# A mixed attention and MLP kernel: transposes moved between token mixing's products, and w4's subtraction moved from POOL to DVE

## The chip, the cores and the metric

One NeuronCore of one Trainium2 chip. The engines are PE (TensorE: products and transposes), ACT (ScalarE), DVE (VectorE), POOL (GpSimd) and SP, whose queue issues the loads. Each takes its instructions in order, and they run beside each other, held together by semaphores. The metric is the device time of one execution in microseconds (us), as the median of several runs.

## The reference

An input x of 2048 tokens by 448 columns goes through two branches, and a gate mixes them per token:

```python
g = _sigmoid((x * gate_w).sum(-1, keepdims=True))
a = _A_ref(x, A_wq, A_wk, A_wv, A_wo)        # 16 query heads of 28, one shared key and value head
b = _B_ref(x, B_w1, B_w2, B_w3, B_w4)
return g * a + (1 - g) * b
```

The branch that matters here is the second one:

```python
h  = _gelu(_layernorm(x) @ w1)                                  # 448 -> 448
hs = concat(four column groups of h, shifted by +1, -1, +2, -2 tokens) @ w2
x1 = x + hs                                                     # token mixing
h2 = _gelu(_layernorm(x1) @ w3) @ w4                            # the MLP, 448 -> 1792 -> 448
return x1 + h2
```

All values are float32.

## The kernel before, in words

**Precision.** PE multiplies in a rounded format. To come close to float32, each operand is kept as two tensors: a high part (names ending in h), a cast by ACT, and a low part (ending in l), which is the raw tensor minus the high part. A product of two operands is three products: high by high, high by low, low by high. So each weight that is loaded goes through the same steps: a DMA into a raw buffer, casts on ACT, a subtraction on DVE or POOL.

**Blocks.** The tokens are four blocks of 512 (`NB` = 4), each of four tiles of 128. The weights w3 and w4 are loaded in seven pairs i = 0 to 6, each of which holds two of the MLP's fourteen hidden chunks f of 128.

**Order.** PE's order is the order of the program. The other engines' order, and that of the loads on SP, is made by a scheduler, which may pull an instruction ahead of others in the program; so an edit of the program's order changes their queues as well.

**The stretch around the change** is the end of the first stage:

- `stage_kv(3)` computes keys and values of the last block, and leaves the values in `vT`. `stage_v(3, vT)` transposes them on PE (tile `vp`); DVE copies the result into `vext` and the gate's sum into `gz`, from which ACT computes `gg` with Exp.
- `ln_begin(0)` takes the statistics of block 0 of x1 on DVE (L126, L127), and POOL makes the factor `rs` (L128, L129).
- `load_w34(i, pool)` loads pair i: `w3raw` (L364), cast by ACT in three pieces (L101, L102, L106), with the low part subtracted by DVE in two (L104, L105); then `w4raw` (L369), cast by ACT (L370) and its low part `w4l` subtracted by POOL (L371). The raw tiles of w3 and of w4 have one buffer each: the load of pair i + 1 cannot start until pair i is cast and subtracted.
- `stage_w2(b)` is token mixing's second product for block b: for each of four tiles t, twelve products into a PSUM tile `hs` of two buffers (L322 to L324), and an addition on DVE that adds it to x1 (L326). It takes a function `between(t)` that is called after each tile.
- `ln_tile(0, t, tp_of)` normalises tile t of block 0: DVE computes `xn` (L135, three buffers), POOL copies its last 64 columns behind it (L137), PE transposes four parts into a PSUM tile `tp` (L140), ACT casts that to `ah` (L109), and DVE makes `al` and a piece of `ah` (L110, L111).

Before the change, block 2's `stage_w2` runs by itself, then come `stage_v(3)`, the loads 1 to 3 in the program's order, the first transposed tile, and block 3's `stage_w2` with the other three transposed tiles between its parts. Those tiles take PSUM buffers of the groups `misc` and `mx`, which have one buffer each.

**Behind the stretch** comes the MLP of block 0. `w3_part(0, f)` makes the product `g_f` (L115 to L119) in a PSUM group `mm` of two buffers; ACT evaluates Gelu on it twice, into `gh` (L409) and `gf` (L410), and DVE makes `gl` from them (L411). So g_2 needs the buffer that `gf_0` frees. `w4_part` (L419 to L421) adds the products with w4 into `acc`, two chunks f later. The loads of pairs 4 to 6 stand at the head of this stage in the program. After the MLP's four blocks comes attention, which takes most of the time and is not touched.

Of the kernel before, what the change touches and what calls it, by code (L numbers as in the profile page):

```python
# [11 lines left out]
ALU = mybir.AluOpType  # L12
# [10 lines left out]
NB = S // 512  # L23
# [12 lines left out]
def f32(ap):  # L36
    return ap.bitcast(F32)
# [3 lines left out]
def gated_mix_kernel(  # L41
# [13 lines left out]
    nc = tc.nc  # L55
# [36 lines left out]
    def misc_tile(name):  # L92
        return psA.tile([P, 512], F32, tag="misc", bufs=1, name=name)
# [5 lines left out]
    def split_w(raw, wh, wl, eng=None):  # L99
        eng = eng or nc.vector  # L100
        nc.scalar.copy(wh[:, 0:3, :], raw[:, 0:3, :])  # L101
        nc.scalar.copy(wh[0:64, 3, :], raw[0:64, 3, :])  # L102
        nc.gpsimd.memset(f32(wh)[64:128, 3, :], 0.0)
        eng.tensor_tensor(wl[:, 0:3, :], raw[:, 0:3, :], f32(wh)[:, 0:3, :], ALU.subtract)  # L104
        eng.tensor_tensor(wl[0:64, 3, :], raw[0:64, 3, :], f32(wh)[0:64, 3, :], ALU.subtract)  # L105
        nc.scalar.copy(wl[64:128, 3, :], raw[64:128, 3, :])  # L106
# [25 lines left out]
    def layernorm_tile(pool, tp_of, b, t, mv, rs, ah, al):  # L132
        xt = x1[:, 4 * b + t, :]
        xn = pool.tile([P, 512], F32, tag="xn", bufs=3, name=f"xn_{pool.name}_{b}_{t}")
        nc.vector.tensor_scalar(xn[:, 0:D], xt, mv[:, t, 0:1], rs[:, t:t + 1],  # L135
                                op0=ALU.subtract, op1=ALU.mult)
        nc.gpsimd.tensor_copy(xn[:, D:512], xn[:, 384:D])  # L137
        tp = tp_of(f"tp_{pool.name}_{b}_{t}").rearrange("p (c n) -> p c n", c=4)
        for c in range(4):
            nc.tensor.transpose(tp[:, c, :], xn[:, c * P:(c + 1) * P], ident)  # L140
        cols = slice(t * P, (t + 1) * P)
        split_a(tp, ah[:, :, cols], al[:, :, cols])
# [60 lines left out]
    with tc.tile_pool(name="s1b", bufs=1) as s1b, \  # L203
# [43 lines left out]
        def stage_kv(b):  # L247
            ah = s1.tile([P, 4, 512], F32R, tag="ah", bufs=2, name=f"ahk_{b}")
            al = s1.tile([P, 3, 512], F32R, tag="al", bufs=2, name=f"alk_{b}")
            if b == 0:  # L250
                for c in range(4):
                    nc.scalar.copy(ah[:, c, :], xraw[b][:, c, :])
                    if c < 3:
                        nc.vector.tensor_sub(al[:, c, :], xraw[b][:, c, :], f32(ah)[:, c, :])
                    else:
                        nc.vector.tensor_sub(ah[64:128, c, :], xraw[b][64:128, c, :], f32(ah)[64:128, c, :])
            else:
                split_a(xraw[b], ah, al)
            xact[b] = (ah, al)
            cols = slice(512 * b, 512 * b + 512)  # L260
            ps = max_tile(f"kv_{b}")[0:64, :]
            proj(ps, kvh, kvl, ah, al)
            nc.scalar.copy(kS[0:32, cols], ps[0:32, :])
            nc.scalar.copy(kS[32:64, cols], ps[0:32, :])
            nc.vector.tensor_sub(kS[64:96, cols], ps[0:32, :], f32(kS)[0:32, cols])
            vT = s1b.tile([32, 512], F32, tag="vT", bufs=1, name=f"vT_{b}")
            nc.scalar.copy(vT, ps[32:64, :])
            return vT

        def stage_v(b, vT):  # L270
            vp = misc_tile(f"vp_{b}")
            for t in range(4):
                nc.tensor.transpose(vp[:, 32 * t:32 * t + 32], vT[:, t * P:(t + 1) * P], ident[0:32, 0:32])
            vp = vp[:, 0:P].rearrange("p (t d) -> p t d", t=4)
            nc.vector.tensor_copy(vext[:, 4 * b:4 * b + 4, 1:1 + DH], vp[:, :, 0:DH])
            nc.vector.tensor_copy(gz[:, 4 * b:4 * b + 4], vp[:, :, DH])
# [40 lines left out]
        def stage_w2(b, between=None):  # L317
            for t in range(4):
                ps = ps1.tile([P, 512], F32, tag="hs", bufs=2, name=f"hs_{b}_{t}")[:, 0:D]
                for m in range(4):  # L320
                    o = 2 + t * P + SHIFTS[m]
                    nc.tensor.matmul(ps, hh[b][0:C, m, o:o + P], w2h[0:C, m, :], start=(m == 0), stop=False)  # L322
                    nc.tensor.matmul(ps, hh[b][0:C, m, o:o + P], w2l[0:C, m, :], start=False, stop=False)
                    nc.tensor.matmul(ps, hl[b][0:C, m, o:o + P], w2h[0:C, m, :], start=False, stop=(m == 3))  # L324
                xt = x1[:, 4 * b + t, :]
                nc.vector.tensor_add(xt, xt, ps)  # L326
                if between:
                    between(t)

        split_w(kvraw, kvh, kvl)  # L330
        vT = stage_kv(0)
# [14 lines left out]
        vT = stage_kv(1)  # L346
# [4 lines left out]
        vT = stage_kv(2)  # L351
        stage_w1(3)
        stage_v(2, vT)
        vT = stage_kv(3)
# [3 lines left out]
        w3h, w3l, w4h, w4l = [], [], [], []  # L358

        def load_w34(i, pool):  # L360
            w3h.append(pool.tile([P, 4, 2 * P], F32R, name=f"w3h_{i}"))
            w3l.append(pool.tile([P, 4, 2 * P], F32R, name=f"w3l_{i}"))
            raw = s2a.tile([P, 4, 256], F32, tag="raw3", bufs=1, name=f"w3raw_{i}")
            nc.sync.dma_start(raw, w3[:, :, i * 256:i * 256 + 256])  # L364
            split_w(raw, w3h[i], w3l[i])
            w4h.append(pool.tile([P, 2, D], F32R, name=f"w4h_{i}"))
            w4l.append(pool.tile([P, 2, D], F32R, name=f"w4l_{i}"))
            raw = s2a.tile([P, 2, D], F32, tag="raw4", bufs=1, name=f"w4raw_{i}")
            nc.sync.dma_start(raw, w4[i * 256:i * 256 + 256, :].rearrange("(c p) n -> p c n", p=P))  # L369
            nc.scalar.copy(w4h[i], raw)  # L370
            nc.gpsimd.tensor_tensor(w4l[i], raw, f32(w4h[i]), ALU.subtract)  # L371

        acts = {}

# [5 lines left out]
        def ln_tile(b, t, tp_of):  # L380
            ah, al, mv, rs = acts[b]
            layernorm_tile(s2a, tp_of, b, t, mv, rs, ah, al)

        ln_begin(0)
        load_w34(0, s2a)
        stage_w2(NB - 2)
        stage_v(3, vT)
        for i in range(1, 4):
            load_w34(i, s2a)
        ln_tile(0, 0, misc_tile)  # L390
        stage_w2(NB - 1, lambda t: ln_tile(0, t + 1, (misc_tile, max_tile)[t % 2]) if t < 3 else None)

    with tc.tile_pool(name="s2", bufs=1, reuse_waits="tile") as s2, \
            tc.tile_pool(name="ps2", bufs=1, space=PSUM, reuse_waits="tile") as ps2:
# [28 lines left out]
        for i in range(4, NF // 2):  # L423
            load_w34(i, s2)
# [385 lines left out]
```

## Time and profile before

| | us |
|---|---|
| median of 3 runs | 1070.64 |
| these runs | 1069.9 to 1074.41 |
| the profiled execution | 1070.98 |
| its span, first to last instruction | 1069.1 |
| mean granted clock of TensorE in it | 0.987 of full speed |
| busy: PE, ACT, DVE, POOL | 1039.7 (97%), 673.2 (63%), 258.0 (24%), 159.8 (15%) |

The profile is of one execution. Its rows name a line of the kernel (L371), the engine, the operation, the tile written and the tiles read. A row of a timeline begins with the start from the span's beginning in us and the duration in us; brackets at its end hold the idle time of the engine before it and what ended that. A row of an operation's summary has durations in ns as minimum, median and maximum. PEld is the loading of PE's weights, SPq is SP's queue of DMA issues. PEclk is the clock that PE was granted as a share of full speed. Numbers of buffers are left out of the names, so `w4l` is each of w4l_0 to w4l_6, and `tp_s2a` is the MLP's transposed tile.

### The profile page before, as it was taken

Reading aid. Unit: us, or ns where it says so; the run is one execution under the profiler, and the core shown is the slowest. Engines: PE = TensorE matmul, PEld = TensorE weight load, DVE = VectorE, ACT = ScalarE, POOL = GpSimd, SP = SyncE. Lnnn points to the kernel's source line nnn. Section 1 sums busy time; section 2 is a strip of 40 time slices with the busy share of each in tenths; the row PEclk is TensorE's granted clock in tenths of the full one; section 3 lists DMA queues with packets and bytes.
Section 4 is the critical chain, followed back from the end, with each engine's and each line's share of the span. In section 5 each row is a group of like instructions: output and inputs, shape, how many; then the busy total and the mean of one; then the engine's idle time right before and its main releaser. Section 6 shows DMA issues by size and latency. Waiting matters only on the chain.

```text
span 1069.1 us, 13948 instructions
## 1 busy us (share of the span) xinstructions
PE 1039.7 (97%) x5610; PEld 679.6 (64%) x5610; DVE 258.0 (24%) x521; ACT 673.2 (63%) x1318; POOL 159.8 (15%) x182
## 2 busy tenths in 40 slices
PE   6999889999999999999999999999999999999995
PEld 4787778888888888454554555554655555555542
DVE  6744952311411311401110110120110210111102
ACT  5444451222222223788888888889888889888873
POOL 5622430110200201603000002010002100000100
PEclk9999899999999999999999999999999999999998
DMA  9401330000000000423211202220202220211001
GB/s 312 131 1 37 111 111 1 1 1 1 1 1 1 1 1 29 164 32 70 33 17 16 31 20 40 39 31 3 39 10 41 39 31 2 40 24 26 10 2 38
DMA packets 30541, 41.15 MB, mean 38 GB/s; under 512 B 8004, under 2 KB 20100, under 8 KB 30340
## 3 DMA queue, kind: packets, MB, share of 16 engines
q1 hardware_dynamic: 30324, 40.04, 16.3%
q8 instruction: 46, 0.75, 0.3%
q14 instruction: 27, 0.22, 0.1%
q10 hardware_dynamic: 144, 0.13, 0.1%
HBM read 23.28 MB, written 3.67 MB: 25 GB/s over the span
## 4 chain that ended last, share of the span: by engine, by line
PE 91%; DVE 4%; DMA 1%; ACT 1%; POOL 1%; issue 1%; SPq 0%; POOLq 0%; ACTq 0%; DVEq 0%
PE s L663 27%; PE pv L625 22%; PE acc L420 4%; PE acc L419 4%; PE acc L421 4%; PE g L115 4%; PE g L116 4%; PE g L117 4%; PE q L503 3%; PE m L166 2%; PE wo L560 1%; PE wo L558 1%; PE wo L556 1%; PE g L119 1%; PE g L118 1%; PE h L116 1%
## 5 line engine op out<-in xcount | busy, mean ns | idle before, releaser
L665 ACT ACTIVATE p<-s 128x512 f32<-128x512 f32 x1024 | 517.6, 627 | 98.1 <-PE s L663 97.8
L663 PE MATMUL s<-qs,kS 98*128 98x512 f32 x1024 | 343.6, 420 | 1.4 <-ACT p L665 0.7
L663 PEld LDWEIGHTS s<-qs,kS 98*128 98x128 f32 x1024 | 181.6, 189 | 168.2 <-ACT p L665 127.1
L625 PE MATMUL pv<-p,vext 128*32 128x512 f32 x2048 | 247.6, 602 | 0.0
L409 ACT ACTIVATE gh<-g 128x512 fp32r<-128x512 f32 x56 | 33.6, 600 | 174.9 <-PE g L119 174.9
L625 PEld LDWEIGHTS pv<-p,vext 128*32 128x32 f32 x2048 | 53.7, 109 | 107.6 <-issue 100.3
L411 DVE TENSOR_TENSOR gl<-gf,gh 128x512 fp32r<-128x512 f32 x56 | 41.3, 738 | 192.1 <-ACT gf L410 192.0
L419 PE MATMUL acc<-w4h,gh 128*128 128x448 f32 x224 | 82.6, 369 | 0.0
L420 PE MATMUL acc<-w4l,gh 128*128 128x448 f32 x224 | 82.0, 366 | 0.0
L421 PE MATMUL acc<-w4h,gl 128*128 128x448 f32 x224 | 81.7, 365 | 0.0
L167 DVE TENSOR_REDUCE mr<-m 128x4 f32<-128x512 f32 x64 | 44.3, 692 | 146.0 <-PE m L166 145.3
L548 POOL CAST onh<-on 128x512 fp32r<-128x512 f32 x15 | 9.2, 614 | 414.8 <-DVE on L545 228.7
L115 PE MATMUL g<-ah,w3h 128*128 128x512 f32 x168 | 67.1, 399 | 3.1 <-ACT gf L410 2.8
L116 PE MATMUL g<-al,w3h 128*128 128x512 f32 x168 | 66.5, 396 | 0.1
L117 PE MATMUL g<-ah,w3l 128*128 128x512 f32 x168 | 66.3, 394 | 0.0
L521 DVE SCALAR_TENSOR_TENSOR good<-rt,good 128x16 f32<-128x16 f32 x15 | 2.6, 175 | 190.2 <-DMA rt<-o 190.2
L419 PEld LDWEIGHTS acc<-w4h,gh 128*128 128x128 f32 x224 | 42.0, 188 | 4.9
L420 PEld LDWEIGHTS acc<-w4l,gh 128*128 128x128 f32 x224 | 42.1, 188 | 4.8
L421 PEld LDWEIGHTS acc<-w4h,gl 128*128 128x128 f32 x224 | 42.0, 188 | 3.6
L166 PEld LDWEIGHTS m<-kS,qs 96*128 96x128 f32 x256 | 38.4, 191 | 6.3 <-DVE mr L167 1.2
L115 PEld LDWEIGHTS g<-ah,w3h 128*128 128x128 f32 x168 | 31.9, 190 | 9.7 <-ACT gf L410 3.3
L564 DVE SCALAR_TENSOR_TENSOR ot<-wo,gg,x 128x448 f32<-128x448 f32 x16 | 10.9, 682 | 108.0 <-PE wo L560 108.0
(204 smaller groups left out, 1144.4 us busy)
## 6 DMA issues: line engine op xcount, KB each, us to landing
qs<-qh SPq DMA_DIRECT2D x32, 256.0 KB
qs<-ql SPq DMA_DIRECT2D x16, 256.0 KB
xq<-in_xT_dram SPq DMA_DIRECT2D x4, 1024.0 KB
x<-in_x_dram SPq DMA_DIRECT2D x4, 896.0 KB
w3raw<-in_w_dram SPq DMA_DIRECT2D x7, 512.0 KB
out_dram<-ot SPq DMA_DIRECT2D x16, 224.0 KB
w4raw<-in_w_dram SPq DMA_DIRECT2D x7, 448.0 KB
xkv<-in_xT_dram SPq DMA_DIRECT2D x3, 1024.0 KB
```

Source lines behind the costliest of these rows:

```text
L115: nc.tensor.matmul(ps, wh[:, c, :], ah[:, c, :], start=(c == 0), stop=False)
L116: nc.tensor.matmul(ps, wh[:, c, :], al[:, c, :], start=False, stop=False)
L117: nc.tensor.matmul(ps, wl[:, c, :], ah[:, c, :], start=False, stop=False)
L166: nc.tensor.matmul(ps[:, j, :], q_of[u][0:96, j, t * P:(t + 1) * P], kS[0:96, 0:MK], start=True, stop=True)
L167: nc.vector.reduce_max(mx_of[u][:, :, t], ps, axis=AX.X)
L411: nc.vector.tensor_sub(gl, gf, f32(gh))
L419: nc.tensor.matmul(ps, gh[:, tok], w4h[i][:, k, :], start=(f == 0), stop=False)
L420: nc.tensor.matmul(ps, gh[:, tok], w4l[i][:, k, :], start=False, stop=False)
L421: nc.tensor.matmul(ps, gl[:, tok], w4h[i][:, k, :], start=False, stop=(f == NF - 1))
L625: nc.tensor.matmul(pv[32 * j:32 * j + 32, :], vext[:, kt, :], ps[j], start=(kt == 0), stop=(kt == NT - 1), tile_position=(0, 32 * j))
L663: nc.tensor.matmul(ps, kS[0:98, kt * P:(kt + 1) * P], q_of[u][0:98, j, :], start=True, stop=True)
L665: nc.scalar.activation(p, ps, AF.Exp, scale=SCALE)
```

## The change

`stage_v(3)` and the four transposed tiles of block 0 move between the products of block 2's `stage_w2`: `stage_v(3)` behind its first tile, transposed tiles 0, 1 and 2 behind the second, third and fourth, and tile 3 right behind that. All four use the group `tp` of two PSUM buffers. Block 3's `stage_w2` then runs by itself, and the loads of pairs 1 to 3 stand behind it in the program. The low parts of all seven pairs of w4 are subtracted by DVE instead of POOL. Nothing that is computed changes.

```diff
@@ load_w34 @@
             nc.scalar.copy(w4h[i], raw)
-            nc.gpsimd.tensor_tensor(w4l[i], raw, f32(w4h[i]), ALU.subtract)
+            nc.vector.tensor_tensor(w4l[i], raw, f32(w4h[i]), ALU.subtract)
@@ end of the first stage @@
         ln_begin(0)
         load_w34(0, s2a)
-        stage_w2(NB - 2)
-        stage_v(3, vT)
+        stage_w2(NB - 2, lambda t: ln_tile(0, t - 1, tp_tile) if t else stage_v(3, vT))
+        ln_tile(0, 3, tp_tile)
+        stage_w2(NB - 1)
         for i in range(1, 4):
             load_w34(i, s2a)
-        ln_tile(0, 0, misc_tile)
-        stage_w2(NB - 1, lambda t: ln_tile(0, t + 1, (misc_tile, max_tile)[t % 2]) if t < 3 else None)
```

The changed kernel is one line shorter, so lines below L390 have numbers lower by one in its profile (Gelu's L409 becomes L408).

## The prediction

> **What bounds the kernel now.** I read the page first, for the engine that ends last, then the list of waits of TensorE from 95 to 260 us, which holds the changed stretch and the MLP's first block, then the chain of work that ended last there, and then each engine's timeline. By the page the chain is PE's:
>
> ```profile
> PE 91%; DVE 4%; DMA 1%; ACT 1%; POOL 1%; issue 1%; SPq 0%; POOLq 0%; ACTq 0%; DVEq 0%
> ```
>
> So this edit can only move the end by moving PE's waits. The list of them (who waited for whom: us in total, times, longest) is short:
>
> ```profile
> PE g L115 <- ACT gf L410: 2.8, 1, 2.8
> PE tp_s2a L140 <- DVE gz L276: 2.7, 1, 2.7
> PE m L166 <- DVE mr L167: 0.5, 2, 0.2
> PE g L115 <- ACT ah L109: 0.3, 1, 0.3
> ```
>
> After the wait for gf_0, PE runs through the MLP's first block. So only the start of the product g_2, which needs the PSUM tile that gf_0 frees, passes to the end; the earlier waits count only if they move gf_0. The chain of waits tells what does (start, us, what):
>
> ```profile
> 124.47 0.84 ACT w4h L370
> 125.39 2.14 POOL w4l L371
> 127.54 3.29 DMA w4raw<-in_w_dram
> 130.88 0.97 issue
> 131.88 2.10 POOL w4l L371
> 134.01 3.34 DMA w4raw<-in_w_dram
> 137.47 0.92 issue
> 138.38 1.28 ACT L409
> 139.68 0.60 ACT gh L409
> 140.28 0.50 ACT gf L410
> 140.82 0.79 PE g L115
> ```
>
> It is the loop of w4's single raw buffer: load, cast on ACT (the "issue" pieces), subtraction on POOL, next load. ACT works in order, and gh_0 and gf_0 stand behind the fifth cast, w4h_4, which began at 137.4. PE, which finished g_1 at 138.0, is early.
>
> **The change, part by part.** The order of instructions of the changed kernel shows ACT's queue as w4h_0, ah_0, ah_1, w3h_1, ah_2, ah_3, w4h_1, w3h_2, w4h_2, w3h_3, table load, gh_0, w4h_3, gf_0. So gf_0 now waits for the fourth pair of weights alone, one w4 round less, and the table load no longer follows the last cast it waits for. From the start of w3h_3 it is casts, table, gh, one w4 cast, gf:
>
> ```profile
> 133.95 0.83 ACT L101 CAST w3h<-w3raw 128x768 fp32r<-128x768 f32 x1 [1.67 <-DMA w3raw<-in_w_dram]
> 134.69 0.40 ACT L102 CAST w3h<-w3raw 64x256 fp32r<-64x256 f32 x1
> 135.12 0.41 ACT L106 CAST w3l<-w3raw 64x256 fp32r<-64x256 f32 x1
> ```
>
> That is 1.6 for the three (133.95 to 135.53), 1.3, 0.5, 0.85 and 0.6, with 0.05 to PE: 4.9 us. The question is when w3raw_3 lands. Against it, w3l_0 moves: on DVE it now stands behind vext, gz and xn_0, and xn_0 waits for rs on POOL.
>
> ```profile
> 109.02 0.94 DVE L104 TENSOR_TENSOR w3l<-w3raw,w3h 128x768 fp32r<-128x768 f32 x1
> 109.88 0.41 DVE L105 TENSOR_TENSOR w3l<-w3raw,w3h 64x256 fp32r<-64x256 f32 x1
> 110.22 0.60 DVE L326 TENSOR_TENSOR x<-x,hs 128x448 f32<-128x448 f32 x1
> 110.86 2.30 DVE L135 TENSOR_SCALAR xn_s2a<-x,mv_s2a,rs_s2a 128x448 f32<-128x448 f32 x1
> ```
>
> ```profile
> 109.01 1.81 POOL L129 TENSOR_TENSOR rs_s2a<-rs_s2a,powt 128x4 f32<-128x4 f32 x1
> ```
>
> ```profile
> L129 POOL TENSOR_TENSOR rs_s2a<-rs_s2a,powt x4: 1007/1007/1813, 109.0 to 202.2; 128x4 f32<-128x4 f32 x4
> ```
>
> Here rs took 1.81 instead of 1.01 while DVE ran L104 and L105, and xn_0 took 2.30 while POOL began its w4l at 110.8: the two engines shut each other out. Without that rs ends at 109.01 + 1.01 = 110.0, xn_0 (448 columns like L326's 0.60, but one input; I take 0.5) at 110.6, L104 and L105 follow with 0.87 + 0.41, and w3raw_0 is free at 111.85 where it was 110.3. The load loop starts 1.55 late.
>
> PE starts the block's first product at 104.58, then vp, then the second product; a product and a transposed tile cost it:
>
> ```profile
> 104.58 0.37 PE L322 MATMUL hs<-w2h,hh 112*128 112x448 f32 x1
> ...
> 126.13 0.60 PE L140 MATMUL tp_s2a<-ident,xn_s2a 128*128 128x128 f32 x4
> 126.48 0.45 PE L322 MATMUL hs<-w2h,hh 112*128 112x448 f32 x1
> ...
> 129.01 0.60 PE L140 MATMUL tp_s2a<-ident,xn_s2a 128*128 128x128 f32 x4
> ```
>
> A tile with its product takes 2.88 (126.13 to 129.01), a product 2.5. PE is at tp_0 at about 110.1 (104.58 + 2 x 2.5 + vp and its wait for vT, half a us) and waits until POOL has copied xn_0's last columns. Between no block by L104 and a full one that copy ends at 110.9 to 112.0; I take 111.9, since L104 starts right behind xn_0. tp_2 then starts at 111.9 + 2 x 2.88 = 117.7, tp_3 at 118.0 and ends at 118.6.
>
> w4l_0 on DVE: the rows of 768 and 256 columns (0.94, 0.41) give 1.04 ns a column, so 896 take 1.07 instead of POOL's 2.1. Seven cost DVE 7.5 us and spare POOL 15. w4l_0 stands behind L326 and three xn, so it ends near 114.7 (111.85 + 0.5 + 3 x 0.45 + 1.07); w4raw_1 follows and, at no more than a w3 load's 4.24 (below), lands at 118.9, when ACT, busy with ah_3 to 119.3, cannot take w4h_1 yet: hidden by 0.4, and past that it would cost what it is late. vp moved ahead of the second product costs PE what it cost behind the fourth, and its wait for vT lies in the wait for xn_0. gg and Exp's table load, now ahead of w4h_0, end that cast at 111.3 (gz at about 108.9, then 1.28, 0.2 and 0.94), 2 us before w4l_0's turn; uncovered they would cost 1.5.
>
> The next w3 round starts late in the same way: DVE takes L105 of w3l_1 behind al and ah of tp_3. ah_3 ends 0.7 after tp_3 (119.3), when one of DVE's two pairs of 0.54 + 0.28 (by that slope) still has 0.3 to go; with the second pair and L105, 120.9. The loads now alternate in SP's queue, w3 ahead of w4; before, it was
>
> ```profile
> 110.36 0.54 SPq L364 DMA_DIRECT2D w3raw<-in_w_dram  x1
> 112.94 7.90 SPq L369 DMA_DIRECT2D w4raw<-in_w_dram  x2
> 120.95 0.55 SPq L364 DMA_DIRECT2D w3raw<-in_w_dram  x1
> ```
>
> ```profile
> 114.60 0.83 ACT L101 CAST w3h<-w3raw 128x768 fp32r<-128x768 f32 x1 [4.88 <-DMA w3raw<-in_w_dram]
> ...
> 126.03 0.83 ACT L101 CAST w3h<-w3raw 128x768 fp32r<-128x768 f32 x1 [0.72 <-DMA w3raw<-in_w_dram]
> ```
>
> A w3 load ahead of its w4 took 4.24 (110.36 to 114.60), one behind it 5.08 (120.95 to 126.03). I take 4.24, as w3 now leads. w3raw_2: issued 120.9, landed 125.15; L101 0.83, L104 0.9, one hs addition 0.5, L105 0.4: w3raw_3 issued 127.9, landed 132.1. Plus 4.9: **g_2 at 137.0, 3.8 before 140.82**. w4_3 is queued behind w3_3: of the pair before, the second w4 issue ended at 120.84 and w3 had landed at 126.03, 5.2 later; I allow 5.6, so 133.5, and w4h_3's turn is at 135.5: covered by 2 us. PE is at g_2 earlier: 129.01 to 138.0 took tp_3, one product, g_0 and g_1; from 118.0 that plus three products more (7.5) is 134.5, so it waits 2.5 us again, and the two waits taken away (2.7, 0.3) gain nothing by themselves. Two new queues stand behind waits. On POOL, the memset of w3h_4 waits for PE's last hs product (about 128.3) and rs of block 1 stands behind it; on DVE block 1's xn and then w3l_3 wait for that rs, to about 132.6 (memsets and rs 2.0, three xn and statistics 2.3): hidden by w3h_3's first cast, at 132.9, and w3l_3 frees only later loads. Behind g_2, DVE has w4l_3 to w4l_6 and w3l_4 to w3l_6 ahead of gl_0 to gl_5. A pair of weights lasts PE two g (5.8, what is left of 129.01 to 138.0 without a tile, a product and the wait of 0.3) and two groups of twelve products like hs's (5.0), and a load round takes 7.0 (120.9 to 127.9): the loads draw ahead by 3.8 a round, which I put at zero cost.
>
> **The clock** is the term that decides. By windows (length; PE, PEld, DVE, ACT, POOL busy; PEclk; DMA, GB/s):
>
> ```profile
> 113.08:116.49 3.41, 1.99 (x12) 1.44 (x10) 3.41 (x11) 1.54 (x3) 1.08 (x3) 1.00 0.71 211
> 116.49:119.91 3.42, 2.14 (x8) 2.04 (x9) 3.42 (x6) 2.85 (x4) 1.89 (x1) 0.51 0.00 1
> 140.39:143.80 3.41, 2.98 (x7) 2.40 (x8) 1.98 (x3) 2.27 (x5) 0.18 (x1) 0.50 0.50 139
> ```
>
> The clock halved after a stretch of 3.41 in which PE was idle 1.42, and again around the gap before g_2, where 2.98 busy us at half clock cost 1.5. The gap that I add at tp_0 lasts 1.8. If these stretches lie at random to it, one of them holds 1.42 of it unless a border falls in its middle 1.04: 1 - 1.04 / 3.41 = 70%. Then a stretch at half clock costs 1.7 before tp_3, and all of that goes through L105 to g_2: 138.7, **2.1 us gained**. The gap before g_2 closes the clock as before, for the same 1.5, so the difference is zero, between -1.5 (open) and +1.5 (a second stretch).
>
> The Trainium skill, "TensorE: Matmul & The Clock Gate", section "What's actually happening", says that the clock falls after at least one idle window of about 3.4 us; by that neither gap would close it, and the sum would be 3.8 + 1.5. The trace does not agree: it halved after gaps of 2.7 and 2.8.
>
> The sum against the profiled execution, 1070.98 (span 1069.1 and 1.9 around it), is 1068.9; the median, 1070.64, lies 0.34 lower, so **1068.5** is the forecast.
>
> **The rivals**, in times of the median.
> - The clock stays up at tp_0 (a border in the middle, or POOL's copy ahead of L104): 3.8 gained, 1066.8.
> - It falls at neither gap: 3.8 + 1.5, 1065.3. For it speaks only that the idle part of a stretch can fall short; against it, both gaps of before.
> - PE bounds g_2: the loads come 2.5 earlier than by my prices, g_2 is at 134.5 with no gap and no half clock: 6.3 + 1.5 = 7.8, 1062.8. Against it, 4.24 is the shortest w3 load that I quote.
> - Slower: the w3 loop becomes longer than the w4 loop was. It decides where w3raw_3 lands after 140.82 - 4.9 = 135.9, 3.8 later than 132.1. A half-clock spell of two stretches at tp_0, as from 116.49 on, where 2.14 busy of 3.42 did not end it, gives 3.4, and loads at 5.08 in two rounds 1.7: landed 137.2, g_2 at 142.1, 1.3 lost, 1071.9.
> - That the change does not do what it says is excluded by the order of instructions.
>
> **How the numbers follow.** Forecast 50%, clock up at tp_0 22%, up at both 8%, PE-bound 5%, slower w3 loop 10%, unnamed 5% (three of them above). The range, 1064.0 to 1072.5, takes in all but PE-bound and unnamed, with half a us or more for the load prices. A measurement of this kernel tells 0.5%, 5.35 us, from no change: below 1065.3 lie PE-bound, half of the clock up at both, some of the third case and one unnamed, 14%; above 1076.0 some unnamed and the far end of the slow loop, 5%; the rest, 81%, is within.
>
> **What the profile after would show.** The wait for gz before tp gone, a wait of some 1.8 at tp_0 for POOL's copy; rs in 1.01; w4l on DVE at 1.07; w3raw_1 issued near 111.9, w3raw_3 near 128 to 130; the first table load for gh right behind w3h_3; g_2 between 137 and 139, still waiting for gf_0; half clock after both gaps. It is wrong if g_2 waits for nothing, if gl_3 or gl_4 make PE wait in the first block, or if w3raw_3 lands after 136.

## The result, and the profile after

| | before | after |
|---|---|---|
| median of 20 runs each, us | 1072.26 | 1068.28 |
| ratio to before | | 0.9973, 95% interval 0.9963 to 0.9983 |
| the profiled execution, us | 1070.98 | 1067.96 |
| its span, us | 1069.1 | 1066.2 |

By the ratio the change gains 2.9 us (1.8 to 4.0 by the interval); the two medians lie 4.0 apart, at the interval's edge, and the runs of each kernel spread over 4.5 to 5.4 us. The measured 1068.28 lies inside the predicted range, and the gain within the half per cent, 5.35 us, that the forecast could not tell from no change. That 1068.28 is so near to the 1068.5 of the forecast is in part luck: the forecast was reckoned from 1070.64, the median of three runs before, and the median of twenty is 1072.26. In the two profiled spans the gain is 2.9 too; what follows accounts for these two executions. How the gain comes about is only partly what the forecast said.

The page of after, its chain by engine:

```profile
PE 92%; DVE 2%; DMA 2%; ACT 1%; POOL 1%; issue 1%; SPq 0%; POOLq 0%; DVEq 0%; ACTq 0%
```

PE still ends last. TensorE's waits from 95 to 260 us in after (who waited for whom: us in total, times, longest):

```profile
PE g L115 <- ACT gf L409: 3.7, 1, 3.7
PE m L166 <- DVE mr L167: 0.5, 2, 0.2
PE tp_s2a L140 <- POOL xn_s2a L137: 0.4, 1, 0.4
PE tp_s2a L140 <- DVE xn_s2a L135: 0.2, 1, 0.2
```

The wait of 2.7 for `gz` is gone. What came at the transposes instead is 0.2 + 0.4, not 1.8, and PE stands longer in front of g_2, 3.7 against 2.8, since it gets there earlier. The chain of waits that leads to g_2 in after (start, us, what):

```profile
120.42 0.29 DVE ah L111
120.73 0.43 DVE w3l L105
121.22 4.06 DMA w3raw<-in_w_dram
125.31 0.85 ACT w3h L101
126.18 0.34 DVE w3l L104
...
127.67 0.34 DVE w3l L105
128.07 4.14 DMA w3raw<-in_w_dram
...
133.82 1.28 ACT L408
135.11 0.60 ACT gh L408
135.73 0.94 ACT w4h L370
136.67 0.51 ACT gf L409
137.22 0.50 PE g L115
```

Before, this chain ran through w4raw and POOL's subtraction. Now it runs through w3raw: load, cast, DVE's two subtractions, next load; then table load, gh_0, one w4 cast, gf_0. g_2 starts at 137.22, 3.6 earlier than the 140.82 of before. (PE's first product of the stretch began 0.3 later in this execution, at 104.92, ahead of anything the change touches; counted from there it is 3.9.)

How the 3.6 passes on is read from the summaries of two operations of PE: the products with w4 (count, ns as minimum, median and maximum, then first and last start) and attention's scores. First of before, then of after:

```profile
L419 PE MATMUL acc<-w4h,gh x224: 362/365/453, 144.8 to 423.3; 128*128 128x448 f32 x112
L663 PE MATMUL s<-qs,kS x1024: 387/397/569, 423.9 to 1049.5; 98*128 98x512 f32 x171
```

```profile
L418 PE MATMUL acc<-w4h,gh x224: 362/365/542, 141.3 to 420.0; 128*128 128x448 f32 x112
L662 PE MATMUL s<-qs,kS x1024: 387/397/632, 420.6 to 1047.6; 98*128 98x512 f32 x171
```

The first product with w4 is 3.5 earlier and the first scores are 3.3 earlier: the MLP passes the gain on whole. But attention, whose code is the same, takes 627.0 from first to last score where it took 625.6. So 1.4 is given back there, 1.0 comes again after the last score (19.6 to the end before, 18.6 after; no run here shows why), and 2.9 is left.

### The profile page after: what moved, and what is told of

The parts are those of the page before. It is cut to its first block, busy times and chain, and to the rows that moved or that the text cites. A ratio compares the mean times of both kernels' runs of the same rounds, so it can differ in the third digit from the quotient of the medians.

```text
span 1066.2 us, 13945 instructions
## 1 busy us (share of the span) xinstructions
PE 1040.3 (98%) x5610; PEld 679.5 (64%) x5610; DVE 258.6 (24%) x528; ACT 673.5 (63%) x1318; POOL 146.1 (14%) x175
## 4 chain that ended last, share of the span: by engine, by line
PE 92%; DVE 2%; DMA 2%; ACT 1%; POOL 1%; issue 1%; SPq 0%; POOLq 0%; DVEq 0%; ACTq 0%
PE s L662 27%; PE pv L624 22%; PE acc L418 4%; PE acc L419 4%; PE acc L420 4%; PE g L115 4%; PE g L116 4%; PE g L117 4%; PE q L502 3%; PE m L166 2%; PE wo L559 1%; PE wo L557 1%; PE g L119 1%; PE wo L555 1%; PE g L118 1%; PE h L116 1%
## 5 line engine op out<-in xcount | busy, mean ns | idle before, releaser
L408 ACT ACTIVATE gh<-g 128x512 fp32r<-128x512 f32 x56 | 33.6, 599 | 175.0 <-PE g L119 174.9
L410 DVE TENSOR_TENSOR gl<-gf,gh 128x512 fp32r<-128x512 f32 x56 | 38.7, 692 | 183.8 <-ACT gf L409 183.8
```

The costliest lines, as they stand in the source:

```text
L410: nc.vector.tensor_sub(gl, gf, f32(gh))
```

## The experiments

Each ratio is to the kernel before, run on the same chip. After's own is 0.9973 (0.9963 to 0.9983).

**Subtraction alone.** The kernel before, with w4's subtraction on DVE:

```diff
-            nc.gpsimd.tensor_tensor(w4l[i], raw, f32(w4h[i]), ALU.subtract)
+            nc.vector.tensor_tensor(w4l[i], raw, f32(w4h[i]), ALU.subtract)
```

> The kernel before, with w4's low parts subtracted on DVE and nothing moved. Theory L (the end follows the start of g_2, and that follows the loads and casts that stand ahead of gf_0 on ACT): in this kernel's order gf_0 again stands behind the fifth pair's cast w4h_4, and w3's rounds start as before, so g_2 starts at 141 plus or minus 1.5 and the ratio to before is 0.999 to 1.002. Theory P (POOL and DVE shut each other out, and the gain is the end of that): nearly all of the gain, 0.997 to 0.998. Theory W (the gain is the removed wait of PE's transposes for gz and its half clock): no change, 1.000, as the transposes stay.

Measured: 1069.71 us, ratio 0.998 (0.9969 to 0.9992). Its chain of waits:

```profile
131.13 1.10 DVE w4l L371
132.25 4.59 DMA w4raw<-in_w_dram
136.87 0.94 ACT w4h L370
137.80 0.51 ACT gf L410
138.35 0.79 PE g L115
```

Here gf_0 still stands behind the fifth w4 cast, as before, and the w4 loop still binds; but its subtraction takes 1.1 instead of 2.1, the loop gets there sooner, and g_2 starts at 138.35, 2.5 earlier than in before. Theory L had put this at nothing, and that was wrong.

**Move alone.** The changed kernel with the subtraction back on POOL:

```diff
-            nc.vector.tensor_tensor(w4l[i], raw, f32(w4h[i]), ALU.subtract)
+            nc.gpsimd.tensor_tensor(w4l[i], raw, f32(w4h[i]), ALU.subtract)
```

> The changed kernel, but with w4's low parts subtracted on POOL as before. Theory L: gf_0 stands behind w4h_3 and the table load behind that cast, and POOL's 2.1 per round instead of 1.07, so g_2 starts at 138 to 139.5, half a us to two later than in the changed kernel, and the ratio is 0.998 to 0.9985: the move carries most of the gain. Theory W: all of the gain, 0.9973, as the place of the transposes is the same. Theory P: little or nothing, 0.9995 to 1.0005, with PE's wait for gf_0 near that of before.

Measured: 1067.27 us, ratio 0.9958 (0.9945 to 0.9971). Its chain of waits (pieces under 0.1 us left out):

```profile
126.39 2.12 POOL w4l L371
128.54 4.09 DMA w4raw<-in_w_dram
132.75 0.92 issue
133.67 1.28 ACT L408
134.96 0.60 ACT gh L408
135.56 0.50 ACT gf L409
136.10 0.50 PE g L115
```

POOL's w4 loop binds, with one round less ahead of gf_0 (the cast at 132.75 is w4h_3). The move alone gains at least as much as both together: the intervals overlap, so the times can't say that it gains more. The profiles, one execution of each, do: counted from the block's first product, g_2 comes 31.6 after it here (104.48 to 136.10) and 32.3 in after. Theory L had put g_2 half a us to two later than in after, so it was wrong here too. With the w4 subtraction on DVE, the end of w3l_1 (L105) stands behind the last `al` and `ah` in DVE's queue, at 120.73; here it runs at 118.21, ahead of them, and w3raw_2 goes out at 118.69 instead of 121.22. So in after the other loop, that of w3, binds. So the two halves of the change reach for the same wait by two ways, and do not add up: counted from that first product, g_2 comes 2.9 us earlier by the subtraction alone, 4.6 by the move alone, and 3.9 by both.

**No gap for the clock.** The changed kernel with 28 products that feed nothing, 256 columns each, put on PE ahead of g_2:

```diff
+                if b == 0 and f == 2:
+                    wps = misc_tile("warm_gap")
+                    for _ in range(28):
+                        nc.tensor.matmul(wps[:, 0:256], warm[:, 0:P], warm, start=True, stop=True)
```

> The changed kernel with 28 products of 256 columns on the warm-up tile between g_1 and g_2, some 3 us of PE work in its gap of 3.7 before g_2 (more work, its result is not used). If the idle gap closes the clock: g_2 starts at 137.2 as in the changed kernel, no half-clock stretch behind it, 1.7 us less, ratio to before 0.9957. If the half clock has another cause: the stretch stays and the ratio is 0.9973. If the extra products run past gf_0, up to 0.5 us is lost again.

Measured: 1065.98 us, ratio 0.9949 (0.9935 to 0.9962). The windows of after around the gap, then one of this kernel (length; PE, PEld, DVE, ACT, POOL busy; PEclk; DMA, GB/s):

```profile
134.50:137.92 3.42, 0.70 (x3) 0.62 (x4) 3.04 (x9) 3.38 (x6) 1.21 (x2) 1.00 0.52 146
137.92:141.33 3.41, 3.41 (x11) 2.62 (x10) 3.35 (x6) 1.77 (x4) 0.00 (x0) 0.54 0.43 147
```

```profile
135.90:139.30 3.40, 2.84 (x17) 2.15 (x16) 3.09 (x6) 2.90 (x5) 1.21 (x2) 1.00 0.63 172
```

g_2 starts at the same time (137.29), but the clock stays at 1.00 behind it, and the first product with w4 comes at 139.9 instead of 141.3. So the half-clock stretch behind the gap costs 1.4, close to the 1.5 of the prediction, and the gap is what closes the clock. The span of this kernel is 3.3 us shorter than after's: 1.4 are this, and 1.5 more are in attention (625.5 from first to last score instead of 627.0), below.

**Loads called later, pair 3 cast on DVE.** The changed kernel with the loads of pairs 3 to 6 called behind g_1 to g_4 in the program, and pair 3's three casts of w3 on DVE, so that gh_0 and gf_0 do not stand behind them on ACT:

```diff
-            split_w(raw, w3h[i], w3l[i])
+            split_w(raw, w3h[i], w3l[i], cast=nc.vector.tensor_copy if i == 3 else None)
...
-        for i in range(1, 4):
+        for i in range(1, 3):
...
-        for i in range(4, NF // 2):
-            load_w34(i, s2)
...
+                if b == 0 and f in (1, 2, 3, 4):
+                    load_w34(f + 2, s2 if f > 1 else s2a)
```

> The changed kernel with the loads of pairs 3 to 6 placed behind g_1 to g_4 in the program, and pair 3's three w3 casts on DVE. In this order gf_0 stands behind w4h_2, no longer behind w3h_3 and w4h_3. Theory L: gf_0 ends at 133.4, just as PE ends g_1, so PE has no wait before g_2 and no half clock behind it: 3.6 + 1.7 us less than the changed kernel, ratio to before 0.992 to 0.9935. Theory W: no further gain, 0.9973, since the transposes stay where they are. If gl_0 or w3l_3 on DVE becomes the next wait, it shows as a wait of acc for gl and the ratio is between.

Measured: 1061.77 us, ratio 0.9905 (0.9889 to 0.992). ACT's timeline of this kernel (start, duration; in brackets the idle time ahead and what ended it):

```profile
128.17 1.28 ACT L409 ACT_TABLE_LOAD   x1
131.48 0.60 ACT L409 ACTIVATE gh<-g 128x512 fp32r<-128x512 f32 x1 [2.02 <-PE g L120]
131.97 0.59 ACT L410 ACTIVATE gf<-g 128x512 f32<-128x512 f32 x1
```

gh_0 now waits for PE's g_0 and for no load. No wait of PE for gf_0 is left, nor a half-clock stretch there, and the first product with w4 starts at 136.3 instead of 144.8. Its time is below both kernels', and lower than theory L had it (0.992 to 0.9935); theory W, by which the gain is that of the transposes, had no further gain here and falls. Which of the two edits brings how much is not separated. Of the 9.1 us between its span (1060.0) and that of before, 8.5 are this start.

**One round fewer by buffers.** The changed kernel with raw buffers of their own for pair 1, so that both loops have one round fewer ahead of g_2:

```diff
+        s1c = ctx3.enter_context(tc.tile_pool(name="s1c", bufs=1))
...
-            raw = s2a.tile([P, 4, 256], F32, tag="raw3", bufs=1, name=f"w3raw_{i}")
+            raw = (s1c if i == 1 else s2a).tile([P, 4, 256], F32, tag="raw3", bufs=1, name=f"w3raw_{i}")
...
-            raw = s2a.tile([P, 2, D], F32, tag="raw4", bufs=1, name=f"w4raw_{i}")
+            raw = (s1c if i == 1 else s2a).tile([P, 2, D], F32, tag="raw4", bufs=1, name=f"w4raw_{i}")
```

> The changed kernel with raw buffers of their own for pair 1, so that its loads start early and both loops have one round fewer before g_2. The queues of ACT put gf_0 behind the casts of pair 3 as a whole. Theory L (the start of g_2 is set by the rounds of the loads through one buffer): w3raw_3 lands one round of 6.9 us earlier, near 125; gf_0 near 130 to 132, before PE finishes g_1 at 133.5; no wait of PE for gf_0, or one under 1 us, no half-clock stretch there, and a ratio to the kernel before of 0.990 to 0.9935. Rival Q (gf_0 waits for ACT's own work, not for the loads): g_2 at 136 or later, ratio 0.9965 or more.

Measured: 1062.05 us, ratio 0.9909 (0.9894 to 0.9925). PE's timeline:

```profile
133.39 0.50 PE L115 MATMUL g<-ah,w3h 128*128 128x512 f32 x1 [0.27 <-ACT gf L412]
```

A second edit that shares only the cause with the one before brings the same 10 us, as theory L had it. That the rounds of the single raw buffers set the start of g_2, and that this start is what counts, is shown.

**Subtraction back on POOL in the better kernel.** The kernel with pair 3 cast on DVE, with w4's subtraction on POOL:

```diff
-            nc.vector.tensor_tensor(w4l[i], raw, f32(w4h[i]), ALU.subtract)
+            nc.gpsimd.tensor_tensor(w4l[i], raw, f32(w4h[i]), ALU.subtract)
```

> The kernel of e6_cast_on_dve (transposes moved, loads of pairs 3 to 6 called behind g_1 to g_4, pair 3's casts of w3 on DVE) with the subtraction of w4's low parts back on POOL. Theory L: once g_2 waits for nothing, neither the w3 nor the w4 loop reaches the end, so that the place of the subtraction is worth nothing: ratio to the kernel before 0.9895 to 0.9915, as the 0.9905 there, and no wait of PE for gf_0. Rival D (DVE's subtraction is what cost the changed kernel its 0.7 us against the move alone, anywhere in the first block): 0.7 us less than there, 0.9895 or below. Rival P (POOL's 2.1 us in w4's round bring the wait back): a wait of 1 us or more before g_2, ratio 0.993 or more.

Measured: 1067.81 us, ratio 0.9956 (0.9939 to 0.9973). PE's timeline and ACT's:

```profile
136.69 0.50 PE L116 MATMUL g<-ah,w3h 128*128 128x512 f32 x1 [2.56 <-ACT gf L410]
```

```profile
133.29 0.94 ACT L371 CAST w4h<-w4raw 128x896 fp32r<-128x896 f32 x1 [6.38 <-POOL w3h L104]
134.25 1.28 ACT L409 ACT_TABLE_LOAD   x1
```

Theory L, which had this at no cost, was wrong again, and the rival with the wait back was right, by two things together whose shares are not separated: with POOL's slower subtraction the scheduler put w4h_3 ahead of gh_0 and gf_0 on ACT, and w4raw_3 went out only at 129.14, when POOL had ended w4l_2 (begun at 127.00, 2.12 long). The row names a memset of POOL as what ended the idle time; that memset isn't read by this cast, and a w4 load of 4.1 issued at 129.14 lands then, so I read it as the load. Added to the move alone, DVE's subtraction gains nothing; here it is worth some 5 us (0.9905 against 0.9956). Its worth depends on which loop is late.

**The gap at tp_0 in one piece.** The changed kernel with the fourth part of the first tile, which needs POOL's copy, transposed first:

```diff
-        for c in range(4):
+        for c in ((3, 0, 1, 2) if pool.name == "s2a" and b == 0 and t == 0 else range(4)):
```

> The changed kernel with one thing else: of the first tile of block 0, PE transposes the fourth part, which waits for POOL's copy of 64 columns, ahead of the other three. In the profile after, PE ran three of the four transposes before that copy and waited 0.23 + 0.41 us instead of the predicted 1.8, and the clock stayed up. Now the whole wait stands in one piece: a gap of 1.6 to 1.8 us that ends near 111.9, as the prediction had it. Theory L (the gap was the failing step, the rest of the sum holds): tp_3 ends 1.1 us later than after, since the three transposes and what follows come behind the copy; w3l_1's last subtraction, the load of w3raw_2 and g_2 follow it by up to that much: g_2 at 137.2 to 138.4 with the clock up, 138.5 to 140 if the gap halves it (by the prediction's 70%). Ratio to the kernel before 0.998 to 0.9995. Rival C (PE's place does not reach the loop, since DVE's queue and not tp_3 holds the load of w3raw_2): g_2 stays at 137.2, ratio 0.9973.

Measured: 1069.06 us, ratio 0.9969 (0.9956 to 0.9981). The waits of PE, and the window that holds the gap:

```profile
PE tp_s2a L140 <- POOL xn_s2a L137: 1.2, 1, 1.2
```

```profile
110.01:113.42 3.41, 2.21 (x14) 1.84 (x13) 3.41 (x8) 1.55 (x3) 1.62 (x2) 1.00 0.15 9
113.42:116.84 3.42, 3.42 (x20) 3.08 (x19) 3.33 (x8) 1.62 (x3) 1.52 (x3) 1.00 0.76 230
```

In one piece the gap is 1.2, less than the 1.42 that closed the clock in before, and the clock stayed up. g_2 starts at 137.19. Counted from the block's first product (104.45) that is 0.4 later than in after, but w3raw_3 was issued 23.2 behind that product in both, and landed 0.4 later here. So the order of the transposes does not reach the loop: rival C.

**alq_0.** Attention's own part of the account. In after the waits of PE behind 260 us hold one that before does not have, and the windows around it show the clock halved behind it:

```profile
PE q L502 <- POOL alq L488: 1.4, 1, 1.4
```

```profile
434.88:438.29 3.41, 2.02 (x11) 1.36 (x9) 0.69 (x1) 2.98 (x7) 3.33 (x2) 1.00 0.57 218
438.29:441.70 3.41, 3.41 (x18) 0.61 (x17) 0.69 (x1) 0.00 (x0) 3.26 (x3) 0.54 0.42 133
```

POOL makes `alq_0`, the low part of attention's first input. The profile of before has a half-clock stretch too, but earlier:

```profile
430.53:433.94 3.41, 3.41 (x17) 0.59 (x9) 3.37 (x4) 1.79 (x4) 2.78 (x3) 0.50 0.19 73
```

It held PE back ahead of this place, and the low part was there in time. Three kernels take alq_0 from POOL to DVE (1.76 there, 3.46 on POOL): the changed one, the one before, and the one with pair 3 cast on DVE, each with this edit:

```diff
-            nc.gpsimd.tensor_tensor(al, raw[:, 0:3, :], f32(ah)[:, 0:3, :], ALU.subtract)
+            (nc.gpsimd if b else nc.vector).tensor_tensor(al, raw[:, 0:3, :], f32(ah)[:, 0:3, :], ALU.subtract)
```

> The changed kernel with the low part of attention's first input, alq_0, computed by DVE behind its cast instead of by POOL behind its other work. In the profile after PE waited 1.4 us for it at 437.5, which the profile before doesn't have: there a stretch at half clock from 430.5 on had put PE 1.7 us behind. Theory S (that wait is how the clock's spells fall in one execution or the other, and belongs to the profile, not to the change): the wait goes, and the ratio gains 0.3 to 1.4 us on the changed kernel's 0.9973: 0.996 to 0.997. Rival N (the half-clock stretch there costs the same with or without the wait, so the end does not move): 0.9973. Rival B (DVE's 1.6 us shut POOL out and delay its later work): 0.9975 or more.

> The kernel before with alq_0, the low part of attention's first input, computed by DVE instead of POOL. On the changed kernel this one edit went from a ratio of 0.9973 to 0.994, and its profile lost both the wait of 1.4 us for alq_0 and the half-clock stretch at 438. Theory I (what alq_0 costs is independent of the change, and falls as a wait in some executions and as a half-clock stretch in others, the profile of before among these): the ratio falls by as much as there, to 0.996 to 0.998, and no stretch near 430 to 440 is left. Theory G (the change alone brought that wait, giving back 1.4 to 3.5 us of its gain): 0.9995 to 1.001, with the half-clock stretch near 430 as in the profile of before.

> The kernel of e6_cast_on_dve (no wait before g_2, ratio 0.9905) with alq_0 computed by DVE. Its profile had no wait for alq_0, but a half-clock stretch at 421.6. Theory I (independent of the rest): 0.9875 to 0.9895, no half-clock stretch between 415 and 440. Theory G (only a kernel whose profile shows the wait gains): 0.990 to 0.991, the stretch stays.

Measured: on the changed kernel 1066.03 us, 0.994 (0.9925 to 0.9955), which is 3.5 us less than after by the ratios; on the kernel before 1070.15, 0.9983 (0.9968 to 0.9997); on the third 1062.0, 0.9906 (0.9888 to 0.9925), no gain. DVE's and PE's timelines in the first of them:

```profile
434.29 1.76 DVE L488 TENSOR_TENSOR alq<-xq,ahq 128x1536 fp32r<-128x1536 f32 x1
```

```profile
436.43 0.39 PE L502 MATMUL q<-alq,wqh 128*128 128x512 f32 x1
```

The wait is gone, the stretch at 438 with it, and attention takes 623.9 from first to last score instead of 627.0. So what after lost in attention is this wait and the clock behind it: shown. How much of it the change brought is not settled. The profiles say that it is bound to neither half of the change: the wait of 1.4 stands in after, in the subtraction alone, in the move alone and in the kernel with the fourth part first (attention 627.0 to 627.1), none of which has a half-clock stretch between 415 and 435 us; the kernels with the gap filled, with pair 3 cast on DVE and with raw buffers for pair 1 have such a stretch, at 421 to 425, and no wait, and so has before, at 430.53 (625.4 to 625.7). The kernel with the subtraction back on POOL stands between: a wait of 0.65, and no stretch up to 440. The kernel before gains 1.8 by the same edit, with no stretch left near 430, so it paid here too; 3.5 and 1.8 lie within each other's errors, and only the two profiles say 1.4. On after the gain is larger than any theory had it, since the half-clock stretch went with the wait. And neither theory of the other two holds as I put it: the kernel before gains, and the third, whose profile has a half-clock stretch near 422 with and without the edit, does not.

## Why the prediction was right, step by step

**What sets the end: right for the MLP, not for attention.** All of g_2's 3.6 reached the first scores but 0.3. That nothing behind could change was wrong by 1.4 in these two executions: a stage that the diff does not touch has a race of its own between PE and POOL, and PE, coming by without the half-clock stretch ahead of it, lost it. The prediction took every wait behind g_2 as fixed.

**The order on ACT and the replay: right.** From the start of w3h_3 to g_2 4.9 was predicted, 4.99 measured (132.23 to 137.22). ACT's timeline and DVE's:

```profile
132.23 0.83 ACT L101 CAST w3h<-w3raw 128x768 fp32r<-128x768 f32 x1 [4.39 <-DMA w3raw<-in_w_dram]
```

```profile
113.87 1.07 DVE L371 TENSOR_TENSOR w4l<-w4raw,w4h 128x896 fp32r<-128x896 f32 x1
```

Less the 0.3 by which this execution was late, the loads fit: w3raw_2 was issued at 121.22 (predicted 120.9), w3raw_3 at 128.07 (127.9), and w4l on DVE took 1.07. rs took 1.01 again, by POOL's timeline:

```profile
109.35 1.01 POOL L129 TENSOR_TENSOR rs_s2a<-rs_s2a,powt 128x4 f32<-128x4 f32 x1
110.97 0.90 POOL L137 COPY xn_s2a<-xn_s2a 128x64 f32<-128x64 f32 x1 [0.61 <-DVE xn_s2a L135]
```

POOL's copy ended at 111.87, where 111.9 was said: it took 0.90 beside DVE's L104, and 0.24 in the median of its sixteen. The Trainium skill, "SBUF — State Buffer", section "Who interferes with whom", says that a DVE instruction with two inputs in SBUF and a GpSimd instruction that reads SBUF shut each other out; these rows agree. g_2 was put at 137.0 with the clock up; it came at 137.22.

**The gap at tp_0: the step that failed.** The forecast took 1.8 of idle time in one piece, with 70% for a half-clock stretch worth 1.7. PE's timeline in after:

```profile
110.96 0.55 PE L140 MATMUL tp_s2a<-ident,xn_s2a 128*128 128x128 f32 x3 [0.23 <-DVE xn_s2a L135]
111.92 0.33 PE L140 MATMUL tp_s2a<-ident,xn_s2a 128*128 128x128 f32 x1 [0.41 <-POOL xn_s2a L137]
```

Two things were wrong in it. PE came at 110.7, not 110.1 (0.3 of it from upstream), so the whole gap is 1.2, as the experiment with the fourth part first measured. And the wait for POOL belongs to one of the four transposes: the other three ran in the gap and left 0.64 idle. By the prediction's own measure, 1.42 idle in one stretch, 1.2 does not close the clock, and in none of the nine profiled kernels with the move does a half-clock stretch lie between 60 and 136 us. So the loss of 1.7 that carried the forecast of 2.1 did not happen. What happened at g_2 is the second case, "the clock stays up at tp_0", 3.8, to which I had given 22%. Of the 3.6 by which g_2 came earlier, 0.3 and attention's 1.4 were lost and 1.0 came again after the last score, which leaves 2.9. The time was right by luck: one loss that was priced did not come, and another that was not priced did.

**The clock behind the gap: right.** It halved for one stretch as in before, at about the same cost. The rule of the Trainium skill that the prediction quotes ("TensorE: Matmul & The Clock Gate", section "What's actually happening"), at least one idle window of about 3.4 us, does not hold here either: by the 0.54 of the window from 137.92 on, the half clock began at 138.2, and in the 3.41 us ahead of that PE was at work for 1.0.

**PE at g_2.** It was there at 133.5, not 134.5. Nothing hung on this but the price of the PE-bound rival: 7.8 us was said, and the two kernels that got there gained 9.8 and 10.2.

**The subtraction: mis-read.** The prediction gave it no term of its own in the gain and tied that to the order on ACT. Alone it is worth 2.9 us at g_2, counted from the block's first product; added to the move it is worth about -0.7.

## What to carry to other kernels

Two edits that shorten the same in-order loop do not add up: find the loop that will be late after the first before pricing the second, and ask what stands in front of the consumer in its engine's queue. When a wait is charged to a group of instructions, ask which of them carries it, since the others may fill the gap. And compare the stages that the edit does not touch as well: a race between two engines that is won by little in one execution, here because a half-clock stretch fell ahead of it, is lost in another, and a part of the gain can go there.

## What the runs showed of the hardware that was not expected

Half-clock stretches of 3.41 us fall on a fixed grid whose place differs from one execution to the next: in before they begin at 116.49, 140.39 and 430.53, which are 7 and 85 steps of 3.413 apart, in after at 138.2 and 438.6. Laid on each execution's own grid, from 60 us to 12 us before the end, the twelve profiles agree on how much work closes the clock: of the stretches at full clock with PE busy for at most 2.02 of the 3.41 us, all but one (1.96) were followed by a stretch at half clock, and none with 2.1 to 3.0 was. A half-clock stretch was followed by a second one in the three cases in which PE was busy for 1.8 to 2.8 of it, and by none where it was busy for 3.0 or more.

Not each half-clock stretch follows idle time of PE that the profile shows. PE was busy all through the window ahead of the one at 430.53 in before:

```profile
427.11:430.53 3.42, 3.42 (x11) 1.33 (x15) 1.41 (x3) 3.42 (x8) 3.33 (x4) 1.00 0.99 382
```

What closed the clock there, and why it stayed up at that place in two of the three kernels in which DVE made alq_0, stays open.
